# One v load of 128 partitions becomes eight of eight partitions and one of 64, in a linear-attention and soft-MoE kernel

## The chip, the cores and the metric

The kernel runs on one core of one Trainium2 chip. The metric is the device time of one execution in microseconds (us), taken as a median over runs; lower is better. Beside it there is a profile of one execution, whose span is counted from the first to the last instruction.

## The reference, cut to what matters

A linear attention with a decaying state feeds a soft mixture of experts.

```python
# r, k, v: (4 batches, 8 heads, 768 steps, 48); w, u: (8, 48)
for t in range(S):
    cur = einsum('bhd,bhe->bhde', u * k[:, :, t], v[:, :, t])
    y[:, :, t] = einsum('bhd,bhde->bhe', r[:, :, t], state + cur)
    state = w[None, :, :, None] * state + einsum('bhd,bhe->bhde', k[:, :, t], v[:, :, t])
x = y as (3072 rows, 384)
logits = x @ phi                                  # phi: (384, 32 slots)
slot_in = softmax(logits, axis=0).T @ x           # 32 slots, 4 for each of 8 experts
slot_out[e] = relu(slot_in[e] @ w1[e]) @ w2[e]    # w1: (8, 384, 1024), w2: (8, 1024, 384)
out = softmax(logits, axis=1) @ slot_out          # (3072, 384)
```

All inputs and the output are float32.

## The kernel before, in words

**Tiling.** Two heads make a pair, 2 x 48 = 96 columns, so each batch has four pairs and the whole has 16 (`nU`). A pair's 768 steps go in two groups of 384, each of three chunks of 128 steps. A loop `for i in range(-5, nH)` runs over the 32 groups and some steps of lead-in. It is a software pipeline written out by hand: in one turn i the group i gets its output, group i+1 its scores, group i+2 its v, and the pairs behind get scaled, transposed and cast. `O(...)` keeps every instruction in the order in which it is written, on each engine.

**Inputs.** The float32 inputs of a batch lie in one of three buffers, `raw[b % 3]`, with k, r and v side by side (`raw_of(which, b)`). Batches 0 to 2 are loaded ahead of the loop, all from SP's queue. The last batch, B - 1 = 3, takes the buffer of batch 0, and its loads stand at turn i == 3 of the loop (lines 557 to 561): `load_kr` (line 117) once for k and once for r, with all eight heads, then `load_v` (line 121) for each pair. They wait for the readers of batch 0's data. A v load puts, for two heads and two groups, a run of 3 steps x 48 values (576 bytes) in each of 128 partitions: 4 runs in each partition. The v of a pair is read by `v_cast` (line 267), which copies it to bf16 on ACT (line 275); for the last pair that is at turn i = 26.

**Weights.** `load_w` (lines 140 and 143) issues one expert's w1 or w2 from POOL's queue, which casts to bf16 on the way. w1 goes to a buffer of its own; w2 goes into `raw[1]` and `raw[2]` once batches 1 and 2 have been used up. The table `W_AT` says at which turn how many of them are issued; ahead of the first, at turn 12, a small POOL copy `guard` waits for the last batch's k. The last expert's w2 comes in three pieces (y rows 0 to 3, 4 to 6, and 7), issued behind the loop.

**The end.** After the loop come the last logits and the dispatch, then the first products with w1, transposes, and `second` (line 661; its matmuls are at line 665), which multiplies with w2, expert by expert: the second group's last two experts are issued on their own, at the end. Then the result is scaled (line 676) and 24 blocks of 128 rows of output are formed (lines 689 to 693) and stored in eight transfers (line 709), from SP and POOL in turn.

**Semaphores of transfers.** The transfers of SP share eight completion semaphores, used in turn; an issue that takes one waits until the one before it on that semaphore has landed.

Of the kernel before, what the change touches and what calls it, by code (L numbers as in the profile page):

```python
# [9 lines left out]
def kernel(  # L10
# [13 lines left out]
    B, H, S, D = r.shape  # L24
# [10 lines left out]
    G = 2  # L35
# [8 lines left out]
    JV = T // C  # L44
# [7 lines left out]
    def O(ins):  # L52
        return tc.keep_in_program_order(ins)

    pe, dve, act, pool, sp = nc.tensor, nc.vector, nc.scalar, nc.gpsimd, nc.sync
# [18 lines left out]
    def raw_of(which, b):  # L74
        return raw[b % NR][:, which * RW:(which + 1) * RW]
# [41 lines left out]
        O(sp.dma_start(out=raw_of(which, b).rearrange("p (h x) -> p h x", h=H)[:, h0:h1, :],  # L117
                       in_=src[b, h0:h1].rearrange("h (p j) d -> p h (j d)", j=J)))

    def load_v(b, h0, h1):  # L120
        O(sp.dma_start(out=raw_of(2, b).rearrange("p (h x) -> p h x", h=H * G)[:, h0 * G:h1 * G, :],
                       in_=v[b, h0:h1].rearrange("h (g p j) d -> p (h g) (j d)", g=G, j=JV)))

    def load_batch(b, step, h=0):
        for h0 in range(h, H, step):
# [123 lines left out]
    def b_pe(m):  # L249
        kT = st["kT", m]  # L250
        for c in range(nC):
            O(pe.transpose(T0[:, c * C:(c + 1) * C], kT[:, c * C:(c + 1) * C], ident[:]))  # L252
# [44 lines left out]
    def a_pe(i):  # L297
        m, b, q, g, n = at(i)
        kT, rT = st["kT", m], st["rT", m]
        for c in range(L):  # L300
            t = slice((g * L + c) * C, (g * L + c + 1) * C)
            for e in range(2):
                s = slice(64 * e, 64 * e + 64)
                O(pe.matmul(Ab[:, e, c * C:(c + 1) * C], kT[s, t], rT[s, t]))  # L304

    def mask_f(i):
        AT = wk.tile([128, 2, L, C], bf, name="AT", bufs=2)
        st["AT", i] = AT
        O(dve.tensor_mul(AT[:], Ab[:, :, 0:T].rearrange("p e (c t) -> p e c t", c=L),  # L309
                         mask_ut[:, None, None, :].to_broadcast([128, 2, L, C])))  # L310
# [39 lines left out]
    def y_pe(i):  # L350
        m, b, q, g, n = at(i)
        AT, vn, rT, Z = st["AT", i], st["v", i], st["rT", m], st["Z", i]
        first = True
        for c in range(L):
            for e in range(2):
                o = c * P2 + e * D
                O(pe.matmul(Yb[:, o:o + D], AT[:, e, c, :], vn[:, c, e, :],  # L357
                            start=first, stop=False, skip_group_check=True))
                first = False
        for c in range(L):  # L360
            if c == 0:
                if g == 0:
                    continue
                z = st["Z0", m]
            else:
                z = Z[:, c - 1, :]
            t = slice((g * L + c) * C, (g * L + c + 1) * C)
            O(pe.matmul(Yb[:, c * P2:(c + 1) * P2], rT[:, t], z, start=False, stop=False,
                        skip_group_check=True))
        O(pe.matmul(Yb[:, 0:L * P2], ident[:], st["dv", i][:].rearrange("p c d -> p (c d)"),  # L370
                    start=False, stop=True, skip_group_check=True))

    def y_evac(i):
        m, b, q, g, n = at(i)
        if q == 0:
            st["x", n] = wk.tile([128, L, Dm], bf, name="x", bufs=4)
        O(act.copy(st["x", n][:, :, q * P2:(q + 1) * P2],  # L377
                   Yb[:, 0:L * P2].rearrange("p (c e) -> p c e", c=L)))
# [31 lines left out]
    def le_t(n, lp=None):  # L410
        Le = st["Le", n]
        lp = le_p if lp is None else lp
        for c in range(L):
            O(pe.transpose(lp[:, c * C:(c + 1) * C], Le[:, c, :], ident[:]))

    def let_ev(n, lp=None, eng=None):
        lp = le_p if lp is None else lp
        if eng is dve:
            O(dve.tensor_copy(LexpT[:, n * T:(n + 1) * T], lp))
        else:  # L420
            O(act.copy(LexpT[:, n * T:(n + 1) * T], lp))

    def disp(n, ds_p, first=True):
        x, Le = st["x", n], st["Le", n]
        for mi in range(nM):
            for c in range(L):
                O(pe.matmul(ds_p[:, mi * ES:(mi + 1) * ES].rearrange("p (j x) -> p j x", j=EG), x[:, c, mi:Dm:nM],
                            Le[:, c, :].rearrange("p (j x) -> p j x", x=32)[:, :, 0:2 * Spe],
                            start=(first and mi == 0 and c == 0), stop=(c == L - 1), skip_group_check=True))
        for c in range(L):  # L430
            O(pe.matmul(ds_p[:, NA - 1:NA], Le[:, c, :], ones[:, 0:1],
                        start=False, stop=(c == L - 1), skip_group_check=True))

    def disp_ev(n, ds_p):
        if n == 0:
            O(dve.tensor_copy(acc[:], ds_p))
        else:
            O(dve.tensor_add(acc[:], acc[:], ds_p))
# [41 lines left out]
    def turn(n, blocks, bank, eng):  # L480
        x, w_ = st["x", n], L * len(blocks) * C
        for b, mi in enumerate(blocks):
            for c in range(L):
                o = (b * L + c) * C
                O(pe.transpose(bank[:, o:o + C], x[:, c, mi * C:(mi + 1) * C], ident[:]))
        dst = xs[:, n - n0, blocks[0]:blocks[-1] + 1].rearrange("p m c t -> p (m c t)")
        if eng is dve:
            O(dve.tensor_copy(dst, bank[:, 0:w_]))
        else:
            O(act.copy(dst, bank[:, 0:w_]))  # L490
# [8 lines left out]
    for i in range(-5, nH):  # L499
        mu, odd = divmod(i, 2)  # L500
        if 0 <= i + 1 < nH:
            a_pe(i + 1)
            mask_f(i + 1)
        if pend:
            disp_ev(*pend.pop())
        if i == nH - 1:
            turn(n0, (2,), Vb[:].bitcast(bf), act)
            disp(n0 - 1, ds_t)
            le_t(n0 - 1)
            let_ev(n0 - 1, None, dve)  # L510
        if 0 <= i < nH:
            y_pe(i)
            y_evac(i)
        if 0 <= i + 2 < nH:
            v_pe(i + 2)
            v_evac(i + 2)
        if 0 <= i + 1 < nH:
            m_pe(i + 1)
            z_evac(i + 1)
        if odd == 0 and 0 <= mu + 1 < nU:  # L520
            prod_f(mu + 1)
        if odd and i > 0 and mu + 2 < nU:
            b_pe(mu + 2)
            b_evac(mu + 2)
        if odd and 0 <= mu + 3 < nU:
            scale(mu + 3, 0)
        if not odd and 0 <= mu + 2 < nU:
            scale(mu + 2, 1)
        route(i, 0)
        if 0 <= mu + 2 < nU:  # L530
            t_pe(mu + 2, odd)
            route(i, 1)
            t_evac(mu + 2, odd)
            if odd and i < 0:
                b_pe(mu + 2)
                b_evac(mu + 2)
        else:
            route(i, 1)
        if odd == 0 and 0 <= mu + 2 < nU:
            v_cast(mu + 2)  # L540
        route(i, 2)
        if i == nH - 3:
            turn(n0, (0, 1), T0, act)
        if i == nH - 2:
            turn(n1, (0, 1), T1, act)
        for f, j, q in T_AT.get(i, ()):
            f(j, q)
        if i in (-4, -3):
            wu_steps(i + 4)
        if i in Z_AT:  # L550
            q = Z_AT[i]
            O(act.activation(out=zt[:, q, 2, :], in_=zt[:, q, 0, :], func=AF.Copy, scale=wT[:, q:q + 1]))
        if i == 2:
            O(pool.memset(ones[:], 1.0))
            for t in Le_t:
                O(pool.memset(t[:], 0.0))
        if i == 3:
            load_kr(0, k, B - 1, 0, H)
            load_kr(1, r, B - 1, 0, H)
            for h0 in range(0, H, 2):  # L560
                load_v(B - 1, h0, h0 + 2)
        if i == 5:
            O(act.copy(phi_b, phi_f))
        if i == 6:
            for mi in range(nM):
                for j in range(nM):
                    o = C * mi - j + nM - 1
                    O(pe.matmul(Xb[:, mi * ES:(mi + 1) * ES].rearrange("p (j g s) -> p j g s", g=2, s=Spe),
                                Q3[:, o:o + C],
                                phi_b[:, j * ES:(j + 1) * ES].rearrange("p (g j s) -> p j g s", g=2, s=Spe),  # L570
                                start=(j == 0), stop=(j == nM - 1)))
            O(act.copy(phi_s[:].rearrange("p m s -> p (m s)"), Xb[:, 0:nM * ES]))
        if i == 28:
            O(pool.memset(uns, 0.0))
        if i == min(W_AT):
            O(pool.tensor_copy(guard[:], raw_of(0, B - 1)[:, 0:1]))
        for _ in range(W_AT.get(i, 0)):
            load_w(nw)
            nw += 1
# [160 lines left out]
```

The softmax here doesn't subtract the row's maximum and nothing guards it: scores larger than these inputs give would overflow.

## Time and profile before

| | |
|---|---|
| median of 8 runs | 121.99 us (121.22 to 122.81) |
| the profiled execution: time | 121.22 us |
| the profiled execution: span | 119.4 us |
| granted TensorE clock | 0.961 |
| busy share of the span | PE 85%, DVE 80%, ACT 70%, POOL 49% |
| DMA packets | 20797, 31.79 MB, mean 266 GB/s |
| SP's and ACT's input queues: packets | q1 17648, q10 170 |
| POOL's queue | 2960 packets, 15.34 MB |

One execution is profiled. An engine is busy while it executes; waiting isn't counted. A chain of waits goes back from the last instruction: at each step to what released it, or to the instruction before it on its engine. The DMA share is the mean busy share of the core's 16 DMA engines; in stretches where packets overlap it can pass 1. An issue by SP is shown as an instruction of SP's queue with the time the issuing took, which includes what it waited for; when its data has landed is told by 16 marks on its completion semaphore, one for each DMA engine's share.

### The profile page before, as it was taken

How to read it: one execution, taken by the hardware profiler on the slowest of the kernel's cores; microseconds unless marked ns; L12 is line 12 of the kernel's file. 1: busy time of each engine (PE TensorE's matmuls, PEld its weight loads, DVE VectorE, ACT ScalarE, POOL GpSimd, SP SyncE). 2: the span in 40 equal slices, each digit the busy share in tenths (PEclk: the TensorE clock that was granted, in tenths of full speed). 3: DMA queues.
4: the chain of work that ended last, by engine and by line, in shares of the span. 5: the costliest groups of instructions: out<-in, count | busy, mean ns of one | idle time of the engine just before them, and what ended most of it. 6: DMA issues, size and time to landing. Idle time of an engine off the chain costs nothing.

```text
span 119.4 us, 4334 instructions
## 1 busy us (share of the span) xinstructions
PE 101.7 (85%) x1795; PEld 82.2 (69%) x1797; DVE 95.1 (80%) x187; ACT 83.7 (70%) x183; POOL 58.8 (49%) x70
## 2 busy tenths in 40 slices
PE   5995987799999999999999999999997999795000
PEld 1444866687888888888878798898785597682000
DVE  6899699999999999899999899999964430499000
ACT  4359869797988898988988997998792520398000
POOL 7417634599999999888677595101000000011100
PEclk9998599999999999999999999999999999999955
DMA  4999999999999999999999999999999998179991
GB/s 112 320 310 372 376 370 373 369 390 363 336 382 382 341 222 226 202 224 207 220 213 216 217 212 220 209 224 206 224 208 222 210 207 161 20 293 390 424 403 70
DMA packets 20797, 31.79 MB, mean 266 GB/s; under 512 B 1129, under 2 KB 17898, under 8 KB 20650
## 3 DMA queue, kind: packets, MB, share of 16 engines
q0 software_dynamic: 2960, 15.34, 57.2%
q1 hardware_dynamic: 17648, 16.03, 39.9%
q8 instruction: 14, 0.23, 0.7%
q10 hardware_dynamic: 170, 0.15, 0.4%
q14 instruction: 5, 0.04, 0.1%
HBM read 39.38 MB, written 4.72 MB: 369 GB/s over the span
## 4 chain that ended last, share of the span: by engine, by line
PE 46%; DMA 23%; DVE 12%; ACT 6%; issue 4%; POOL 1%; POOLq 0%; DVEq 0%; ACTq 0%
DMA raw<-in_moe_w_dram 21%; PE T L240 7%; PE Vb L289 7%; PE Ab L304 5%; PE Yb L357 4%; PE T L252 3%; PE Mb L330 3%; DVE prod L262 2%; PE Yb L370 2%; DVE raw L691 2%; PE Yb L149 2%; PE Xb L392 2%; DMA LexpT<-in_w_dram 2%; PE Xb L385 2%; DVE AT L309 2%
## 5 line engine op out<-in xcount | busy, mean ns | idle before, releaser
L233 POOL TENSOR_TENSOR kr<-raw,W 128x576 bf16<-128x576 f32 x30 | 41.9, 1414 | 14.8 <-ACT W L197 6.1
L309 DVE TENSOR_TENSOR AT<-Ab,mask_ut 128x768 bf16<-128x768 f32 x32 | 30.5, 952 | 0.8 <-PE Ab L304 0.6
L289 PE MATMUL Vb<-v_bf,Q 128*128 128x96 bf16 x288 | 17.8, 208 | 0.0
L240 PE MATMUL T<-ident,kr 128*128 128x128 bf16 x192 | 16.7, 226 | 1.3 <-POOL kr L233 1.3
L289 PEld LDWEIGHTS <-Q 128*128 128x128 bf16 x288 | 15.9, 99 | 1.5 <-issue 0.2
L246 ACT COPY kT<-T 128x768 bf16<-128x768 bf16 x16 | 12.8, 800 | 4.4 <-PE T L240 3.2
L246 ACT COPY rT<-T 128x768 bf16<-128x768 bf16 x16 | 12.8, 800 | 4.1 <-PE T L240 3.4
L262 DVE TENSOR_TENSOR prod<-T,kT 128x768 bf16<-128x768 bf16 x16 | 15.3, 953 | 0.0
L347 DVE TENSOR_TENSOR dv<-vn,Mb 128x288 bf16<-128x288 bf16 x32 | 14.3, 447 | 0.0
L346 DVE TENSOR_TENSOR Z<-Mb,zt 128x288 bf16<-128x288 f32 (+1 forms) x32 | 12.9, 402 | 1.1 <-ACT vn L295 0.5
L240 PEld LDWEIGHTS <-kr 128*128 128x128 bf16 x192 | 12.3, 100 | 2.1 <-POOL kr L233 1.4
L295 ACT CAST vn<-Vb 128x288 bf16<-128x288 f32 x32 | 13.4, 418 | 0.1
L377 ACT CAST x<-Yb 128x288 bf16<-128x288 f32 x32 | 13.1, 410 | 0.2 <-PE Yb L370 0.2
L709 POOL DMA_DIRECT2D out_dram<-W x1 | 0.5, 549 | 25.1 <-DVE W L691 25.1
L304 PE MATMUL Ab<-rT,kT 64*128 64x128 bf16 x192 | 11.1, 222 | 2.0 <-DVE AT L309 1.9
L330 PE MATMUL Mb<-vn,kn 128*128 128x96 bf16 (+2 forms) x80 | 11.5, 242 | 0.0
L357 PE MATMUL Yb<-vn,AT 128*128 128x48 bf16 x192 | 10.3, 185 | 0.1
L275 ACT CAST v_bf<-raw 128x576 bf16<-128x576 f32 x15 | 10.2, 678 | 0.0
L304 PEld LDWEIGHTS <-kT 64*128 64x128 bf16 x192 | 5.6, 95 | 5.6 <-DVE AT L309 1.9
L357 PEld LDWEIGHTS <-AT 128*128 128x128 bf16 x192 | 7.1, 96 | 3.3
L370 PE MATMUL Yb<-dv,ident 128*128 128x288 bf16 x32 | 9.1, 284 | 0.2
L257 DVE COPY kn<-T 128x768 bf16<-128x768 bf16 x16 | 8.9, 554 | 0.4 <-PE T L252 0.4
(143 smaller groups left out, 216.3 us busy)
## 6 DMA issues: line engine op xcount, KB each, us to landing
w_all<-in_moe_w_dram POOLq DMA_DIRECT2D x8, 768.0 KB, 12.7
raw<-in_moe_w_dram POOLq DMA_DIRECT2D x7, 768.0 KB, 17.9
raw<-in_v_dram SPq DMA_DIRECT2D x12, 288.0 KB, 6.1
raw<-in_r_dram SPq DMA_DIRECT2D x8, 288.0 KB, 5.8
raw<-in_k_dram SPq DMA_DIRECT2D x2, 1152.0 KB, 9.9
raw<-in_r_dram SPq DMA_DIRECT2D x2, 1152.0 KB, 9.8
raw<-in_k_dram SPq DMA_DIRECT2D x7, 288.0 KB, 6.2
out_dram<-raw POOLq DMA_DIRECT2D x1, 1536.0 KB, 6.7
```

Of the source, the lines that this page charges most:

```text
L233: O(eng.tensor_mul(kr[:, j].rearrange("p j (h s) -> p j h s", s=64)[:, :, :, 0:D], src, W[j][:, q].rearrange("p j (h d) -> p j h d", h=2)))
L240: O(pe.transpose(bank[:, x * C:(x + 1) * C], kr[:, j, x, :], ident[:]))
L246: O(act.copy(t[:].rearrange("p (s j) -> p s j", j=J), bank[:, 0:S].rearrange("p (j s) -> p s j", j=J)))
L262: O(dve.tensor_mul(pr[:].rearrange("p (s j) -> p s j", j=J), T1[:, 0:S].rearrange("p (j s) -> p s j", j=J), st["kT", m][:].rearrange("p (s ...
L289: O(pe.matmul(Vb[:, c * P2:(c + 1) * P2], Q3[:, o:o + C], vb[:, :, g, j, :], start=(j == 0), stop=(j == JV - 1)))
L295: O(act.copy(vn[:].rearrange("p c e d -> p (c e d)"), Vb[:, 0:L * P2]))
L304: O(pe.matmul(Ab[:, e, c * C:(c + 1) * C], kT[s, t], rT[s, t]))
L309: O(dve.tensor_mul(AT[:], Ab[:, :, 0:T].rearrange("p e (c t) -> p e c t", c=L), mask_ut[:, None, None, :].to_broadcast([128, 2, L, C])))
L330: O(pe.matmul(o, kn[:, g * L + c, :], vc, start=first, stop=True, skip_group_check=True))
L347: O(dve.tensor_mul(dv[:], st["v", i][:].rearrange("p c e d -> p (c e) d"), Mb[:, 288:288 + 2 * L, None].to_broadcast([128, L * 2, D])))
L357: O(pe.matmul(Yb[:, o:o + D], AT[:, e, c, :], vn[:, c, e, :], start=first, stop=False, skip_group_check=True))
L377: O(act.copy(st["x", n][:, :, q * P2:(q + 1) * P2], Yb[:, 0:L * P2].rearrange("p (c e) -> p c e", c=L)))
```

## The change

The v of the last pair of the last batch (heads 6 and 7 of batch 3) is no longer one load of 128 partitions. Partitions 64 to 127 come in eight loads of eight partitions each, in order, and after them partitions 0 to 63 in one load. `load_v` gets a range of partitions for that. The destination, the data and the runs of 576 bytes stay as they were. Everything else stands as before.

```diff
-    def load_v(b, h0, h1):
-        O(sp.dma_start(out=raw_of(2, b).rearrange("p (h x) -> p h x", h=H * G)[:, h0 * G:h1 * G, :],
-                       in_=v[b, h0:h1].rearrange("h (g p j) d -> p (h g) (j d)", g=G, j=JV)))
+    def load_v(b, h0, h1, p0=0, p1=128):
+        O(sp.dma_start(out=raw_of(2, b).rearrange("p (h x) -> p h x", h=H * G)[p0:p1, h0 * G:h1 * G, :],
+                       in_=v[b, h0:h1].rearrange("h (g p j) d -> p (h g) (j d)", g=G, j=JV)[p0:p1]))
...
         if i == 3:
             load_kr(0, k, B - 1, 0, H)
             load_kr(1, r, B - 1, 0, H)
-            for h0 in range(0, H, 2):
+            for h0 in range(0, H - 2, 2):
                 load_v(B - 1, h0, h0 + 2)
+            for p0 in range(64, 128, 8):
+                load_v(B - 1, H - 2, H, p0, p0 + 8)
+            load_v(B - 1, H - 2, H, 0, 64)
```

## The prediction

> **What bounds the kernel now.** I read the page first, then the chain of waits, then a table of stages, then the timeline of the queue that the edit touches. The page's rows of slices (40 slices of 2.99 us) show how full the transfer engines are:
>
> ```profile
> span 119.4 us, 4334 instructions
> ...
> DMA  4999999999999999999999999999999998179991
> GB/s 112 320 310 372 376 370 373 369 390 363 336 382 382 341 222 226 202 224 207 220 213 216 217 212 220 209 224 206 224 208 222 210 207 161 20 293 390 424 403 70
> ```
>
> The DMA engines are at nine tenths from the second slice to the 33rd, so for a hundred microseconds there is no hole. Two streams fill that time. Up to slice 14 (41.8 us) it is the inputs on SP's queue, at some 370 GB/s; after that it is the weights, issued by POOL and cast to bf16 on the way, at some 215 GB/s of what is written. Then the chain of waits, in order of time:
>
> ```profile
> 76.76 0.37 issue
> 77.13 25.10 DMA raw<-in_moe_w_dram
> 102.28 0.24 PE Xb L665
> 103.06 0.43 DVE W L676
> ```
>
> The last 25.10 us before the tail are one wait for the second weights. PE's last expert at L665 starts when a weight transfer lands. From 102.28 on there is only the tail: the last products, the scaling, and 24 blocks of output. So the end is (landing of the last weights) + 17 us, and the landing is a matter of how much work each of the 16 DMA engines has to do. The table of stages says it again; its last two columns are the DMA share and GB/s:
>
> ```profile
> core 0: us, PE busy (x) PEld busy (x) DVE busy (x) ACT busy (x) POOL busy (x), PEclk, DMA share, GB/s
> ...
> 38.80:43.20 4.40, 4.38 (x91) 3.81 (x90) 4.40 (x10) 4.04 (x9) 4.36 (x6) 1.00 1.15 308
> 43.20:77.10 33.90, 33.65 (x685) 28.86 (x682) 32.75 (x63) 29.72 (x69) 24.78 (x27) 1.00 1.04 215
> 77.10:102.30 25.20, 23.38 (x489) 19.14 (x486) 14.60 (x33) 14.19 (x32) 1.06 (x2) 1.00 1.00 203
> ```
>
> A share of 1.00 to 1.15 (packets overlap a little) means that nothing can be put on these engines for nothing. Until 77 us PE, DVE and ACT are nearly full too, but the weights, not they, end last. At last the edited place, SP's own timeline and the reader of what it loads on ACT's:
>
> ```profile
> 24.14 5.80 SPq L117 DMA_DIRECT2D raw<-in_k_dram  x1
> 30.04 1.67 SPq L117 DMA_DIRECT2D raw<-in_r_dram  x1
> 31.76 6.70 SPq L121 DMA_DIRECT2D raw<-in_v_dram  x4
> 104.34 0.83 SPq L709 DMA_DIRECT2D out_dram<-raw  x2
> ```
>
> ```profile
> 79.72 0.68 ACT L275 CAST v_bf<-raw 128x576 bf16<-128x576 f32 x1
> ```
>
> The four v transfers of the last batch are SP's last inputs; after 38.46 SP has nothing to issue until 104.34. The cast of the last pair comes at 79.72, some 36 us after that pair landed (43.16, from the completion marks of the trace). So the time at which this v arrives is worth nothing; only the work that it puts on each engine can count.
>
> [...]
>
> **The change part by part.**
>
> *Bytes and packets.* The last pair's v is 128 partitions x 4 runs of 576 B = 512 packets in both kernels, 32 per engine before. Its cost comes from the marks: the last batch's four v transfers landed at 40.68, 41.52, 42.49 and 43.16, so 2.48/3 = 0.83 us each, 26 ns per packet per engine. After the change, engines 0 to 7 carry eight pieces x 4 packets + 16 packets of the 64-partition rest = 48; engines 8 to 15 carry 16. So 16 packets x 26 ns = 0.42 us move from one half of the engines to the other. Each of engines 0 to 7 also writes 9 completion packets instead of 1: 8 x 9 ns (the duration of a four-byte packet) = 0.07 us. Sum: +0.49 us on engines 0 to 7, -0.42 us on 8 to 15; the total is unchanged but for the marks.
>
> *SP's issues.* Nine in place of one. A small issue took 0.37 us at the start of the span; one v issue took about 1.7 us here[...]. Also, the program has eight completion semaphores for SP's transfers, used in turn, and an issue waits until the earlier user of its semaphore has landed. By the order of the built program the pieces wait in turn for k of batch 2, r and v of batch 2, k of batch 3 (landed 36.66), r (39.80), then the three v transfers (40.68, 41.52, 42.49), and the last 64 partitions for the first piece. So the last issue goes out at about 43 us and lands at about 45 to 46, not 43.16. Queued behind it on SP: only the outputs at 104.34. What hides it: 34 us up to the cast at 79.72. Engines that lack v packets meanwhile work on weights, whose first packets start at 41.0 us and whose queue never runs dry (first weights landed at 46.63, when three more had been issued). Price: 0. Without that cover it would be the 2 to 3 us.
>
> *Waits of readers.* The cast waits for eight semaphores instead of one. These are extra semaphore instructions on ACT, 17 ns each by the row of SP's own at L121: 7 x 17 ns = 0.12 us, 22 us before the weights land and with ACT at 0.56 of its time in that stage. The first output on SP collects eight semaphores as well, all long complete. Price: 0.
>
> *What is late next.* The landing is that of the slowest of 16 engines. The sixteen marks of the last weight transfer (the 96 KB one) are 100.10, 100.22, 100.64, 100.93, 100.94, 101.13, 101.21, 101.23, 101.30, 101.40, 101.44, then a gap, then 102.33, 102.52, 102.64, 102.66, 102.74. Five engines come 0.9 us behind the other eleven. If any of the top two or three is one of engines 0 to 7, the end moves by +0.3 to +0.49. If all five are among 8 to 15, they come in at 102.32, while the best of the others rises to at most 101.93: the end moves by -0.42. The spread comes from stalls that hit single engines: 14 packets of 16 KB (instruction fetches, about 1 us each, one every 6 to 7 us) and three reads of 0.86 to 1.19 us among the inputs between 6 and 8 us. Nothing in these says that they prefer the upper half. With five late engines drawn from 16, the chance that none lies in the lower half is 56/4368, 1%; I give it far more, since what picks the engines isn't seen and may be systematic.
>
> *Sum.* +0.4 us on the landing, one for one on the end. The profiled execution took 121.22 us (span 119.4, 1.8 around it): 121.6. It was the fastest of the eight runs, whose median is 121.99; on the median that makes 122.4.
>
> **Rivals.**
>
> *The late engines are all in the upper half* (-0.42, 121.57): for it, a gap of 0.9 us between two groups, which looks like something systematic, and moving 0.42 from one half to the other would nearly close it. Against it, the late group is five and not eight, and the single stalls explain it.
>
> [...]
>
> *Nothing happens* (122.0): the pieces are spread over 16 engines after all, or the stalls fall on other engines in every run and swamp the shift. A read of 1 us is twice the shift; the eight runs spread over 1.6 us.
>
> **How the numbers follow.** Slower by the shift, around 122.4: 0.45. Faster by it, around 121.6: 0.30. No change: 0.10. [...] A measurement of this kernel can tell about 0.5% (0.6 us) from no change, and the shift itself is 0.35%, so most of the chance lies within. Faster by over 0.5% (below 121.4) takes the far side of the second case, 0.19; slower by over 0.5% (above 122.6) takes the fourth case and the far side of the first, 0.31; within, 0.50. The range is 121.4 to 123.0; the likeliest case alone has 122.1 to 122.6.
>
> **What would show it.** In the profile after: nine v issues at the edited line, reaching to about 43 us; about 64 more four-byte packets on q1 (8 more marks x 8 engines, so some 17,712 packets, up from 17,648); the chain still ending in the wait for the weights; marks of the last weight transfer reaching to about 103.2 if I am right, to 102.3 if the first rival is; 576-byte packets still about 29 ns long around 40 to 45 us[...]. I am wrong if the end of the weights moves by more than 0.5 us either way with these packet times unchanged, or if the tail after the weights changes.

## The result, and the profile after

| | before | after |
|---|---|---|
| median of the runs | 121.73 us (56 runs) | 122.39 us (19 runs) |
| the profiled execution: time | 121.22 us | 122.06 us |
| its span | 119.4 us | 120.2 us |

The ratio is 1.0059, with a 95% interval of 1.0041 to 1.0076: slower by 0.66 us on the medians. The forecast was 122.4, which was 0.4 over the 121.99 of the first eight runs of the kernel before; over 56 runs that kernel's median is 121.73.

The page's rows of slices, after:

```profile
span 120.2 us, 4345 instructions
...
DMA  4999999999999999999999999999999999079991
GB/s 109 309 341 358 374 378 369 376 391 360 341 381 378 265 208 225 219 221 212 218 216 213 220 211 218 213 214 219 212 219 210 221 202 171 16 276 382 401 442 70
```

The row of digits shows nothing: nine tenths all the way, as before. The row under it does: the 14th slice (39 to 42 us) moved 341 GB/s before and 265 now. The ten slices on either side differ by 17 GB/s at most. The chain of waits, from 77 us on:

```profile
77.86 25.15 DMA raw<-in_moe_w_dram
103.00 0.04 issue
103.05 0.24 PE Xb L668
...
103.82 0.43 DVE W L679
```

It is the same chain, 0.77 us later: PE's last expert starts at 103.05 instead of 102.28. The wait itself is as long as before (25.15 against 25.10). That suggests that the loss happened ahead of 77 us, and that the stage from 77 us to the end only carries it on. The completion marks say it more firmly. For each weight transfer I take the mean of its sixteen marks, after minus before:

| weight transfer | 1st | 2nd | 3rd | 4th | 5th to 18th |
|---|---|---|---|---|---|
| mean of its marks before, us | 45.77 | 49.49 | 53.15 | 56.88 | 60.56 to 101.46 |
| after minus before, us | 0.00 | 0.27 | 0.56 | 0.72 | 0.69 to 0.83 |

The first weights land when they did before. The loss comes in between 46 and 58 us and doesn't grow after that. The table of stages (the last two columns are the DMA share and GB/s) shows a change still earlier:

```profile
38.80:43.20 4.40, 4.38 (x91) 3.72 (x89) 4.40 (x10) 3.92 (x9) 4.36 (x6) 1.00 1.06 258
43.20:77.10 33.90, 33.65 (x685) 29.00 (x683) 32.76 (x63) 29.96 (x69) 25.18 (x28) 1.00 1.04 216
77.10:102.30 25.20, 23.34 (x490) 19.08 (x490) 14.94 (x34) 14.31 (x32) 1.06 (x2) 1.00 1.02 208
```

In the stage in which the weights start, 258 GB/s move instead of 308, with a DMA share of 1.06 instead of 1.15. SP's queue, from its timeline and from the list of the instructions of L121 between 29 and 60 us:

```profile
31.82 11.71 SPq L121 DMA_DIRECT2D raw<-in_v_dram  x12
105.11 0.87 SPq L712 DMA_DIRECT2D out_dram<-raw  x2
```

```profile
L121 SPq DMA_DIRECT2D raw<-in_v_dram x12: 272/299/1764, 31.8 to 42.8; - x12
```

The nine issues reach to 43.53, as forecast (about 43). But the data is far later than forecast: by the completion marks the eight pieces landed at 42.50, 42.68, 42.87, 43.06, 45.39, 47.38, 49.80 and 51.78, and the 64 partitions at 59.18, not at 45 to 46. The DMA queues between 43.5 and 60 us, first before, then after, show what goes on there. The columns are packets, MB and share of 16 engines; q0 is POOL's queue, which carries the weights, and q1 is SP's:

```profile
q0 software_dynamic: 642, 3.51, 103.4%
q8 instruction: 2, 0.03, 0.7%
```

```profile
q0 software_dynamic: 607, 3.34, 97.8%
q1 hardware_dynamic: 414, 0.21, 6.0%
```

Before, SP's queue has nothing there. After, 414 of its packets (366 of v, the rest completion marks) go between packets of weights, and 35 fewer packets of POOL's queue get through. The trace names no engine, but the distances between starts of weight packets pile up at about 456 ns where weights are alone, and at about 493 ns while v packets are among them. So a late v packet cost some 37 ns, and one in a row of its kind 26.

Each piece left nine marks and not sixteen: one at its issue and eight as the data came (38.56, then 40.87 to 42.50 for the first); the 64 partitions left sixteen. Taken in order, the eight marks of the first four pieces follow each other from piece to piece by 0.17 to 0.21 us, and the sixteen of the 64 partitions, which come last, fall into two groups of eight: 54.26 to 55.62 and 57.52 to 59.18. From this I read that the pieces ran on eight engines, the same eight each time. Which eight, no trace names: the 0 to 7 and 8 to 15 of the prediction and the expectations stand for the eight with the pieces and the other eight.

**A theory.** The three v transfers that go ahead of it, and the last pair's v, are what SP's queue gives the DMA engines while POOL's first weights come up. In the kernel before, all of it is in the queue in time. In the changed kernel three quarters of the last pair's v is not: the last four pieces and the 64 partitions land between 45.39 and 59.18. So engines run dry soon after 41 us, which I call the hole (the DMA share is 0.82 and 0.93 in the two half microseconds from 41.5 us on, against 1.21 and 1.09 before), and later the missing packets come among weights, at 37 ns instead of 26. To size it I give each packet of the trace the time that it holds its engine (456 ns for a weight packet, 47 for an input packet of 1152 bytes and 26 for one of 576, by the distances of their marks, and 0.9 us for an instruction fetch) and call the rest of the engines' time unheld, as a mean over 16 engines. This is an account, not a measurement. Between 40.5 and 43.5 us it is 0.13 us before and 0.66 after. That is +0.53; with 366 late v packets x 11 ns / 16 = +0.25 it makes +0.78. The mean of the sixteen marks of the last weight transfer moved from 101.46 to 102.20, +0.74, and its last mark from 102.74 to 103.50, +0.76. The account closes, but it has a weak point. It comes from one profile of each kernel, and the first weights were issued at 38.80 us in the one and at 39.14 in the other. The edit touches nothing on POOL. How much of the 0.53 comes from these 0.34 us isn't known.

**Rivals.** The skew of the prediction (by the counts of marks, eight engines carry 8 x 4 + 16 = 48 packets of the last pair's v and the other eight 16). Crowding, a guess that no trace shows: packets that go into neighbouring partitions at the same time slow each other down. Between 40.5 and 43.5 us the 576-byte packets took 29 ns in the median in both kernels. A third is the moment at which the weights happened to be issued in the profiled execution.

### The profile page after: what moved, and what is told of

Read it like the earlier page. It is cut to its first block, busy times and chain, and to the rows that moved or that the text cites. A ratio compares the mean times of both kernels' runs of the same rounds, so it can differ in the third digit from the quotient of the medians.

```text
span 120.2 us, 4345 instructions
## 1 busy us (share of the span) xinstructions
PE 101.5 (84%) x1795; PEld 81.8 (68%) x1797; DVE 96.5 (80%) x187; ACT 83.8 (70%) x183; POOL 59.3 (49%) x70
## 3 DMA queue, kind: packets, MB, share of 16 engines
q1 hardware_dynamic: 17712, 16.03, 39.8%
HBM read 39.38 MB, written 4.72 MB: 367 GB/s over the span
## 4 chain that ended last, share of the span: by engine, by line
DMA 36%; PE 31%; DVE 15%; POOL 4%; issue 3%; ACT 2%; POOLq 1%; DVEq 0%; ACTq 0%
DMA raw<-in_moe_w_dram 34%; PE T L240 5%; PE Vb L289 5%; POOL kr L233 4%; DVE raw L694 3%; PE Ab L304 3%; PE Yb L357 3%; DVE prod L262 2%; PE T L252 2%; PE Mb L330 2%; PE Yb L149 2%; DVE AT L309 2%; DMA LexpT<-in_w_dram 2%; PE Yb L370 2%; DVE W L193 2%
## 5 line engine op out<-in xcount | busy, mean ns | idle before, releaser
L401 ACT COPY xT<-Xb 128x384 bf16<-128x384 bf16 x18 | 8.7, 485 | 0.2 <-PE Xb L392 0.2
```

## The experiments

| run | what | ratio to before, 95% interval | unheld us, 40.5 to 43.5 | first weights issued, us |
|---|---|---|---|---|
| before | the kernel before | 1 | 0.13 | 38.80 |
| after | the change | 1.0059 (1.0041 to 1.0076) | 0.66 | 39.14 |
| e1_strided | pieces of partitions four apart | 1.0034 (1.0000 to 1.0067) | 0.06 | 37.90 |
| e2_sixteen | eight pieces of 16 | 1.0051 (1.0028 to 1.0075) | 0.72 | 39.38 |
| e3_late_whole | one transfer, late | 1.0088 (1.0058 to 1.0117) | 0.37 | 39.73 |
| e4_early_skew | skew in time | 1.0022 (1.0006 to 1.0039) | 0.75 | 39.27 |
| e5_no_last_v | last v left out | 0.9957 (0.9938 to 0.9977) | 0.83 | 39.47 |
| e6_halves | two halves | 1.0054 (1.0032 to 1.0077) | 0.80 | 39.66 |
| e7_rest_first | 64 partitions first | 1.0057 (1.0036 to 1.0079) | 0.79 | 39.52 |
| e8_merged | three pairs in one, last whole | 0.9997 (0.9966 to 1.0027) | 0.09 | 39.08 |
| e9_after_w_early | after, weights a turn earlier | 1.0035 (1.0006 to 1.0065) | 0.14 | 38.08 |
| e10_before_w_early | before, weights a turn earlier | 0.9998 (0.9968 to 1.0029) | 0.08 | 37.82 |
| e11_skew_w_early | e4, weights a turn earlier | 1.0049 (1.0026 to 1.0072) | 0.30 | 37.84 |
| e12_sixteen_w_early | e2, weights a turn earlier | 1.0012 (0.9988 to 1.0037) | 0.10 | 38.01 |

The last two columns are from one profile each; the ratios, from 6 to 22 runs of each kernel against 47 to 70 of the kernel before (56 for the change), are the sturdier column. The unheld time goes with the issue of the weights. Where that is at 38.1 us or before, it is 0.30 us at most; from 39.14 on it is 0.37 to 0.83. In e1 the weights came early (37.90) though nothing in its edit touches them. Kernels with the last pair's v whole and in time (before, e8, e10) have no hole at any of their issue times, 37.82 to 39.08. So both the missing v and the later weights belong to the hole, and the column can't tell them apart.

**e1_strided: no crowding.**

```diff
-            for p0 in range(64, 128, 8):
-                load_v(B - 1, H - 2, H, p0, p0 + 8)
+            for p0 in range(64, 128, 32):
+                for s0 in range(4):
+                    load_v(B - 1, H - 2, H, p0 + s0, p0 + 32, 4)
```

If crowding were the cause, pieces of partitions four apart would win most of the 0.6 us back: 1.000 to 1.002, by the author's estimate.

> The eight pieces are kept, but each takes eight partitions four apart (64, 68, ..., 92 and so on)[...]. Same bytes, packets, engines and issues. [...] Late pieces (a hole at the start of the weights and dearer packets between weights) and skew between engines: nothing changes, ratio 1.005 to 1.007.

The ratio of 1.0034 lies between the estimate for crowding and the expectation for the others, and its interval touches both. The kernel isn't the same but for the spacing, either: an issue took 0.68 us instead of 0.30, and v packets went on until 73.8 us. This run leaves crowding undecided.

**e2_sixteen: late, no skew.**

```diff
-            for p0 in range(64, 128, 8):
-                load_v(B - 1, H - 2, H, p0, p0 + 8)
-            load_v(B - 1, H - 2, H, 0, 64)
+            for p0 in range(0, 128, 16):
+                load_v(B - 1, H - 2, H, p0, p0 + 16)
```

> The last pair's v comes in eight pieces of 16 partitions, one partition for each of the 16 engines: every engine has 32 packets again, as before, but the pieces wait for the same semaphores and go out as late as in the changed kernel. Skew: the loss is gone, ratio 0.999 to 1.001. Late pieces: the loss stays or grows a little (16 to 20 late packets on all engines, 8 marks each), +0.5 to +0.8 us, ratio 1.004 to 1.007. [...]

The ratio is 1.0051, with 512 packets in even pieces, 32 to an engine if each piece of 16 partitions is spread over all sixteen. (In e12, which has the same pieces, the packets of SP's queue between 43.5 and 60 us are by their number and bytes some 396 of v and 112 marks, 7 x 16.) So a loss of this size doesn't need the skew.

**e3_late_whole: late, in one piece.**

```diff
-            for p0 in range(64, 128, 8):
-                load_v(B - 1, H - 2, H, p0, p0 + 8)
-            load_v(B - 1, H - 2, H, 0, 64)
+            fill = cst.tile([1, 7 * 24], f32, name="fill")
+            for n in range(7):
+                O(sp.dma_start(out=fill[:, n * 24:(n + 1) * 24], in_=w[n:n + 1, 0:24]))
+            load_v(B - 1, H - 2, H)
```

> The last pair's v comes in one transfer of 128 partitions as before, but seven transfers of 96 bytes (part of w, never read) stand ahead of it on SP and take its turn of semaphores, so that it waits for the third v transfer (42.5 us) and goes out behind the start of the weights. No skew, no pieces, no crowding. Late pieces: +0.5 to +0.8 us, ratio 1.004 to 1.007, with 32 packets per engine found between weight packets, and a hole between 41 and 42.5 us. Skew [...]: ratio 0.999 to 1.001.

The ratio of 1.0088 is the worst of all and above the expected range, though its interval reaches into it. It is the same transfer as before, in one piece, only late. SP issued it at 43.32 and it landed 20.6 us later. Of all runs this one shows best that lateness by itself costs enough; what the seven small transfers ahead of it cost was not measured alone. The marks show the loss building up as in the changed kernel: the first weights land 0.45 us later than before, the fifth 1.74. (Its profile had also a pause of SP's queue before 38.8 us, so its hole is not to be compared to the others to the tenth.)

**e4_early_skew and its control e8_merged.**

```diff
-            for h0 in range(0, H - 2, 2):
-                load_v(B - 1, h0, h0 + 2)
-            for p0 in range(64, 128, 8):
-                load_v(B - 1, H - 2, H, p0, p0 + 8)
-            load_v(B - 1, H - 2, H, 0, 64)
+            load_v(B - 1, 0, H - 2)
+            load_v(B - 1, H - 2, H, 0, 80)
+            for p0 in range(80, 128, 8):
+                load_v(B - 1, H - 2, H, p0, p0 + 8)
```

> The first three pairs' v is one transfer; the last pair's comes as partitions 0 to 79 (16 engines, 5 each) and six pieces of eight partitions, which by the order of semaphores wait for nothing later than r (39.8 us), so all go out before the weights start. Engines 0 to 7 have 44 packets and 8 to 15 have 20: three quarters of the changed kernel's skew, without the lateness. Skew: +0.3 to +0.4 us, ratio 1.003. Late pieces: 0 to -0.2 us, ratio 0.999 to 1.001. [...]

```diff
-            for h0 in range(0, H - 2, 2):
-                load_v(B - 1, h0, h0 + 2)
-            for p0 in range(64, 128, 8):
-                load_v(B - 1, H - 2, H, p0, p0 + 8)
-            load_v(B - 1, H - 2, H, 0, 64)
+            load_v(B - 1, 0, H - 2)
+            load_v(B - 1, H - 2, H)
```

> Control for the early skew: the first three pairs' v in one transfer and the last pair's whole, no pieces. If skew made the 0.2% of the early skew run, this one is at 1.000 (0.999 to 1.001). If the merged transfer made it (fewer, larger issues let SP's queue run out earlier), this one is at 1.002 too.

The ratio is 1.0022 for the early pieces and 0.9997 for the control. So merging costs nothing that these runs can tell (0.3% either way), and the early skewed pieces cost something, less than the change. That is near what skew was to cost (1.003), and three quarters of the loss, the author's estimate for crowding (1.004), lies barely outside the interval. But e4 isn't free of the hole: it has 0.75 us, with all issues out by 40.5. Being early didn't keep the engines busy here, which my theory doesn't explain; e6, below, points to a reason.

**e5_no_last_v: without the load.** The last pair's v isn't loaded.

```diff
-            for p0 in range(64, 128, 8):
-                load_v(B - 1, H - 2, H, p0, p0 + 8)
-            load_v(B - 1, H - 2, H, 0, 64)
```

> Leaves out the load of the last pair's v of the last batch (that pair is computed with the v of batch 0 that still lies in the buffer). 32 packets per engine, 0.83 us, go away, and with them the work that covers the start of the weights. Cover theory (the DMA engines are fed only slowly in the first 1.5 us of the weights, and the last v transfer fills that time): most of the gain is lost to a hole of about 0.5 us, ratio 0.996 to 0.999. If the engines' work alone counts: -0.83 us, ratio 0.993. Unheld time per engine between 40.5 and 43.5 us: 0.6 by the first, 0.1 by the second.

The ratio of 0.9957 is a gain of 0.52 us out of the 0.83 that the engines had to carry. The interval excludes the 0.993 of work alone (barely: 0.9938), so about 0.3 us of that load (0.07 to 0.55 by the interval) was time that the engines lose anyway when the weights start. The queues between 40.5 and 43.5 us, for this run and then for the control e8:

```profile
DMA packets 314, 0.58 MB, mean 194 GB/s; under 512 B 15, under 2 KB 242, under 8 KB 313
## 3 DMA queue, kind: packets, MB, share of 16 engines
q0 software_dynamic: 71, 0.44, 87.0%
q1 hardware_dynamic: 242, 0.13, 14.3%
```

```profile
DMA packets 828, 0.82 MB, mean 274 GB/s; under 512 B 28, under 2 KB 763, under 8 KB 828
## 3 DMA queue, kind: packets, MB, share of 16 engines
q0 software_dynamic: 65, 0.40, 65.3%
q1 hardware_dynamic: 763, 0.42, 47.2%
```

With 521 fewer packets of SP's queue, only 71 packets of weights get through in these 3 us, against 65. They take longer instead: a share of 16 engines over 3 us is 48 us of engine time, so 87.0% x 48 / 71 = 588 ns each, against 482. But the window overstates this, as the weights were issued at 39.47 here and at 39.08 in e8. In the first 4 us after their issue it is 70 packets against 52. The profiled execution of e5 was also one of its slowest (121.74 us, median 121.32). So the first weights use a part of what SP's queue leaves free, and not all of it. By the ratio, somewhat over a third of the load costs nothing there.

**e9 and e10: the weights a turn earlier**, in the changed kernel and in the one before.

```diff
-    W_AT = {12: 1, 13: 1, 14: 1, 15: 1, 17: 1, 19: 1, 20: 1, 22: 1, 23: 1, 25: 1, 26: 5}
+    W_AT = {11: 1, 12: 1, 13: 1, 14: 1, 17: 1, 19: 1, 20: 1, 22: 1, 23: 1, 25: 1, 26: 5}
```

> The changed kernel with the first four weights issued one turn earlier each (turns 11 to 14 instead of 12 to 15), so that the slow start of the weights falls under the first three v transfers. Cover theory: the hole of 0.5 us is filled, and only the dearer packets (37 instead of 26 ns between weights, 0.2 to 0.3 us) stay: ratio 1.001 to 1.003. Skew [...]: no change, 1.005 to 1.007.

> The kernel before with the same earlier issue of the first four weights. Cover theory: the start of the weights was covered already (0.13 us of unheld time there), so 0 to -0.1 us, and more v packets come between weights (up to +0.2): ratio 0.999 to 1.002. If the earlier issue were a gain of its own, this run shows it: below 0.998.

The hole is filled in both (0.14 and 0.08 us), the changed kernel keeps 1.0035, and the kernel before gains nothing. The 1.0035 is a little over the expectation, and its interval overlaps that of the change itself.

**e12 and e11: the same earlier weights with e2 and with e4.** The edit of `W_AT` is that of e9.

> The eight pieces of 16 partitions (late, no skew) with the first four weights a turn earlier: neither hole nor skew, only v packets among weights at 37 instead of 26 ns, 20 to 30 of them per engine, +0.2 to +0.3 us, ratio 1.001 to 1.003. If late packets among weights cost nothing: 1.000. If the hole is not what the earlier issue removes: 1.005 as the run without it.

> The early skew run (44 packets on engines 0 to 7, 20 on 8 to 15) with the first four weights a turn earlier, so that the hole it showed (0.75 us per engine) is filled and the skew is left alone. Skew counts as the prediction had it: ratio 1.002 to 1.004. If skew does not set the end (the cover theory alone): 0.999 to 1.001.

With no other edit than the earlier weights, e2's 1.0051 becomes 1.0012 in e12. The intervals overlap a little, but the marks show how it comes about. The first weights of e12 land 0.66 us ahead of those of the kernel before, and the late v packets take that back: from the fourth transfer on it is 0.02 to 0.12 us behind. So weights that are there early use the time that late v packets leave free. (In e1's profile, with weights as early, the first ones land 0.83 us ahead.) e11 went the other way from e4, from 1.0022 to 1.0049, with a hole of 0.30 left. Of the three kernels with earlier weights and a split v, the two with skew stand at 1.0035 and 1.0049, and the one without at 1.0012. That points to the skew, but doesn't show it. The intervals overlap, and the pieces of e12 differ from the others in size as well, 16 partitions instead of eight.

**e6 and e7: the order of parts.**

```diff
-            for p0 in range(64, 128, 8):
-                load_v(B - 1, H - 2, H, p0, p0 + 8)
-            load_v(B - 1, H - 2, H, 0, 64)
+            load_v(B - 1, H - 2, H, 64, 128)
+            load_v(B - 1, H - 2, H, 0, 64)
```

> Control for the splitting alone: the last pair's v in two transfers, partitions 64 to 127 and then 0 to 63, each on 16 engines. Both wait for semaphores long free, so both go out in time. Cover theory and skew: no change, ratio 0.999 to 1.001. If splitting or half-range transfers cost by themselves: above 1.002.

```diff
-            for p0 in range(64, 128, 8):
-                load_v(B - 1, H - 2, H, p0, p0 + 8)
-            load_v(B - 1, H - 2, H, 0, 64)
+            load_v(B - 1, H - 2, H, 0, 64)
+            for p0 in range(64, 128, 8):
+                load_v(B - 1, H - 2, H, p0, p0 + 8)
```

> The changed kernel with the 64-partition transfer ahead of the eight pieces. The same packets on the same engines, but 16 of them per engine (0.42 us) now go out in time and cover part of the start of the weights. Cover theory: hole of about 0.2 instead of 0.66 us and only some 20 late packets on engines 0 to 7, ratio 1.001 to 1.004. Skew: as the changed kernel, 1.005 to 1.007.

Both missed what the cover theory said of them. e7's 1.0057 is where the skew alone would have put it, but e6 has no skew and costs as much. It was to change nothing and stands at 1.0054, with almost no lateness (the second half landed at 44.04, against 43.16), no skew and no small pieces. The queues between 40.5 and 43.5 us, for before, for the change and for e6:

```profile
DMA packets 765, 0.81 MB, mean 269 GB/s; under 512 B 29, under 2 KB 696, under 8 KB 765
## 3 DMA queue, kind: packets, MB, share of 16 engines
q0 software_dynamic: 69, 0.42, 70.4%
q1 hardware_dynamic: 696, 0.38, 43.3%
```

```profile
DMA packets 386, 0.62 MB, mean 206 GB/s; under 512 B 28, under 2 KB 314, under 8 KB 385
## 3 DMA queue, kind: packets, MB, share of 16 engines
q0 software_dynamic: 71, 0.44, 80.1%
q1 hardware_dynamic: 314, 0.16, 21.3%
```

```profile
DMA packets 776, 0.67 MB, mean 224 GB/s; under 512 B 45, under 2 KB 731, under 8 KB 776
## 3 DMA queue, kind: packets, MB, share of 16 engines
q1 hardware_dynamic: 731, 0.40, 66.6%
q0 software_dynamic: 45, 0.28, 52.6%
```

Per q1 packet that is, by the same working, 43.3% x 48 / 696 = 30 ns before, 33 after and 44 in e6. In e6 about as many v packets as before take half as long again; over its 731 packets the 14 ns more are 0.64 us per engine, an estimate of about the size of its loss. (That only 45 weight packets come through beside them is mostly their later issue, 39.66: in the first 4 us after it there are 49, and 45 before.) The packets of e4, e7 and e11, which also split the last pair's v and send half of it or more in time, cost 42, 41 and 42 ns by the same working; those of the remaining runs 28 to 34. So the slower packets go with a split of a v that is in time; why they are slower isn't shown, and nothing else was tried on it. In the change itself this is not the main thing: its packets are 33 ns in this window, and there are only 314 of them. The marks tell the two kernels apart as well. In e6 the first weights already land 0.73 us later than before, and nothing is added after; in the changed kernel it is 0.00 at first and grows while v packets are among the weights. e7 has both slower packets (41 ns, as in e6) and late pieces.

## Why the prediction was right

The side and the range held. The number held by luck, twice over. The 122.4 is 0.4 over a median of 121.99, and 122.39 was measured, but the kernel before is at 121.73 over more runs, so the slowdown was 0.66 us: base and shift were each off by 0.26, and the two errors cancel. And most of what makes up the 0.66 isn't what the forecast counted. Its own sign of being wrong came up: the end of the weights moved by more than 0.5 us (0.76), with packets of SP's queue at 33 ns in the mean, near the 29 that it named. By its steps:

- *What bounds the kernel*: right. The end is the landing of the last weights plus about 17 us (103.50 and 120.2), and the wait in the chain is as long as before. That nothing can be put on full engines for nothing is too strong: leaving out a load of 0.83 us gained 0.52 (e5).
- *Bytes and packets*: right as to the count. q1 has 17,712 packets, as forecast, 64 more than before, and each piece left eight marks for its data.
- *The skew moves the end by +0.3 to +0.49*: not what made most of the loss. The marks of the last weights moved as a whole: the mean by 0.74, the last by 0.76. Had half of the engines got 0.49 more and half 0.42 less, the mean would have stayed. The marks aren't further apart, either: 2.6 us from first to last before, 2.5 after. e2, without skew, loses about as much. A part of the skew may be in e9 and e11.
- *SP's issues, price 0*: this step failed. It had the waits for semaphores and the issue times right, and named the cover for the reader of v, but said that engines without v packets "work on weights". For a time there were too few weights to work on: between 40.5 and 43.5 us 71 weight packets went through, and 69 before, though 382 fewer packets of SP's queue stood beside them. The first weights landed no earlier for it, and the v packets still had to be carried later. The v transfer was itself the cover. By the account the price is +0.53 us of unheld time, part of which may be the later issue of the weights, and +0.25 for late packets at 37 instead of 26 ns. The step also put the last landing at 45 to 46 us; it was 59.18, as v packets went out no faster than about one for each weight packet (in e3, one in 494 ns on each engine).
- *Waits of readers, price 0*: no run speaks against it; the chain doesn't touch them.
- *Crowding* (the fourth case, 122.7 and above at 0.15, a guess that no trace carried): not the main cause here. It looked at the pieces; slower packets show best in two plain halves (44 ns in e6), and what makes them slow isn't shown.
- *The late engines all in the upper half*: no; the end moved the other way.

Open: how much of the 0.66 us is skew (e12 against e9 and e11 leave 0 to 0.45 us), how much of the hole is the edit's and how much that of the profiled execution, and why e4 lost only 0.22% with a hole as deep as the others'. Why the first weights come up slowly wasn't tried.

## What to carry to other kernels

A transfer that nobody waits for can still be worth its place (in e5, leaving out 0.83 us of it gained 0.52): look at what the DMA engines would do in that stretch without it, and don't take a queue that has been issued for a queue that can be served at once (here 1.5 us passed from the issue at 39.14 to the first packet at 40.61). Where transfers take completion semaphores in turn, count the issues: nine in place of one push the later ones behind the landing of the earlier (the eighth piece went out at 42.50, when the third v transfer had landed at 42.48). Before splitting a transfer by partitions, try the plain halves: here they alone cost as much as the whole change (1.0054 against 1.0059).

## What was not expected of the hardware

- A 576-byte packet among 6144-byte weight packets went out about once per weight packet: in e3 the 512 packets of the last pair, 32 for each engine, started between 46.9 and 62.7 us, one in 494 ns. In a row they took 0.83 us, by the marks of the kernel before.
- The first weights came up slowly where they came late. In the changed kernel, e2, e4, e5, e6 and e7 their first packet started 1.46 to 1.52 us after the issue, and the longest of the first dozen or so took 1.05 to 1.36 us; later ones took 0.47. In e10, e11 and e12, where they came among more packets of SP's queue, nearly all took 0.47 from the first on.
- Two transfers of 64 partitions were slower than one of 128 with the same bytes: 44 against 30 ns a packet in this stretch, and 0.54% of the kernel.
